# One instruction list exchanged for another: gated linear attention and a gated feed-forward on one core

## The chip, the cores and the metric

One core of a Trainium2 chip runs the whole program. The metric is the time of one execution on the device in microseconds (us). The kernel before took 240.67 us as the median of three runs (240.0 to 240.79).

## The reference

The first half is a linear attention with a complex decay for every channel, over 4 batches, 8 heads, 768 tokens and 48 channels a head. The second half is a gated feed-forward block on the 3072 tokens of 384 channels that come out of it.

```python
mag = np.sqrt(a_re * a_re + a_im * a_im)
scale = np.minimum(mag, 0.999) / (mag + 1e-06)
a_re_n, a_im_n = (a_re * scale, a_im * scale)
for t in range(S):                                   # per batch and head, state S is 48 x 48
    new_re, new_im = ar * S_re - ai * S_im, ar * S_im + ai * S_re
    S_re, S_im = new_re + outer(k[t], v[t]), new_im
    y[t] = q[t] @ S_re
x = y as [tokens, 384]
out = x + sigmoid(x @ w_res) * ((gelu(x @ w_gate) * (x @ w_val)) @ w_out)
```

## The kernel before

The tokens of a batch are cut into six chunks of 128. A **unit** is one or two (batch, chunk) blocks of the same chunk that are worked on together. There are 14 units: P0 and P1 hold one block each of chunk 0, P2 two; P3 to P10 hold two blocks each of chunks 1 to 4; P11 holds two of chunk 5, P12 and P13 one each. A unit p goes through three stages, and the names below are P3, A3, F3 for the stages of unit 3.

**Prepare (P).** SP loads ar, ai, q, k, v (`load`, L420, 192 KB for one block). The decay is summed over the tokens in logarithm and angle. ACT takes the logarithm of ar (`ln`, L442, tile la) and its inverse (`exp`, L443, tile t), t is multiplied by ai (`tai`, L445), squared (`sq`, L448 on ACT, L450 elsewhere, tile s), ACT takes the logarithm of 1 + s (L451), DVE adds it to la and caps it (L452, L456). TensorE (PE) sums la over the tokens with a triangular matrix (L406 in fp32 for units 0 to 2; L402 in two narrower pieces for the others, which need `lv`, L460, tile ll, and `tl`, L517). ACT turns the sums into exp and exp of the negative (L487 to E, L488 to Ei). The angle is ACT's arctangent of t (`atan`, L497); the last angle of the chunk before comes to it by a small DMA (`carry`, L503, L509); PE sums it, `round` (L524 on ACT, L527 on DVE) and `fr` (L529) bring it into range, `abs` (L536 on ACT, L538 on DVE), and ACT takes sine and cosine (`sin`, L542, tile CS). q times E and k times Ei (`qe`, L548, tiles Qe, Ke) times CS (`feat`, L553) are the features, transposed on PE with a copy out of PSUM (L569; `cpT`, L377 on ACT, L378 elsewhere), from unit 6 on by DMA (`dT`, L562). `vcast` brings v into bf16; `mrd`, `mrc` and `Mc` bring the last row of E to the state's layout (L492, L377 or L378, tiles mr, M).

**Attend (A).** PE multiplies features (`qk`, L610), DVE masks the product (`am`, L615), PE multiplies it with v and adds the state's share (`av`, L626, L628), `x` copies the result, `kv` (L642), `U`, `Gf`, `Gb`, `Gbc` (L665, L672, L678, L685) carry the state on.

**Forward (F).** x is transposed on PE with a copy (L708, `cpX`, tile xT), from unit 10 on by DMA (`dX`, L702). PE multiplies with the gate and the value weights (L726, tiles wg, wv: six groups of 12 matmuls for one block, twelve groups of 6 for two), ACT takes the gelu (L736), DVE multiplies (`h`, L737, tile hb), PE multiplies with the output weights (`out`, L761) and the residual gate (L748, ACT's tanh L751), DVE multiplies (`ot`, L765), `otx` adds x (L768), SP stores (L770).

Thirty groups of four matmuls on constants (`warm`, L777) stand among PE's work in the front. The weights are loaded in 16 pieces issued by POOL (L384; wg and wv in six pieces each).

ACT computes from one table at a time: logarithm and exp ("L"), arctangent and sine ("T"), gelu and tanh ("G"). Each change is an ACT_TABLE_LOAD (L785).

All 1418 steps are recorded first and numbered in the order in which the code records them. A table `PLACE` says for some steps by their number on which engine they run, and a list `ORDER` says in which order all are issued:

```python
def place(default):
    return PLACE.get(len(plan.steps), default)
...
for j in order:
    t = self.steps[j]
    ...
    x.index = min(range(x.bufs), key=lambda i: row[i])
    ...
    if t.act is not None and t.act != table:
        table = t.act
        load(table)
    ins = t.fn()
```

An engine works through its steps in the order of the list and waits at each for what it needs. Buffers, PSUM banks (8) and table loads follow from the list too.

Of the kernel before, what the change touches and what calls it, by code (L numbers as in the profile page):

```python
# [47 lines left out]
    54: "POOL", 65: "DVE", 67: "DVE", 70: "POOL", 77: "DVE", 80: "ACT", 120: "POOL", 128: "ACT", 133: "DVE", 144: "ACT",  # L48
    146: "ACT", 152: "DVE", 157: "ACT", 190: "DVE", 191: "DVE", 202: "DVE", 208: "DVE", 210: "DVE", 218: "ACT", 220: "DVE",
    224: "DVE", 233: "DVE", 239: "DVE", 242: "DVE", 245: "DVE", 247: "ACT", 303: "POOL", 307: "POOL", 315: "DVE", 319: "POOL",  # L50
    322: "DVE", 324: "DVE", 326: "DVE", 330: "POOL", 336: "DVE", 355: "DVE", 420: "DVE", 421: "POOL", 425: "POOL", 433: "ACT",
    436: "POOL", 439: "DVE", 441: "DVE", 443: "DVE", 447: "POOL", 457: "DVE", 458: "ACT", 460: "ACT", 466: "DVE", 475: "DVE",
    482: "ACT", 538: "POOL", 542: "POOL", 550: "ACT", 553: "POOL", 558: "DVE", 560: "DVE", 564: "POOL", 570: "DVE", 574: "DVE",
    577: "ACT", 589: "DVE", 592: "DVE", 640: "DVE", 667: "ACT", 670: "POOL", 673: "DVE", 675: "DVE", 677: "DVE", 680: "POOL",
    681: "POOL", 690: "ACT", 696: "DVE", 702: "DVE", 753: "DVE", 780: "ACT", 783: "POOL", 790: "DVE", 794: "POOL", 801: "ACT",
    809: "DVE", 815: "DVE", 818: "DVE", 822: "DVE", 823: "DVE", 881: "POOL", 885: "POOL", 893: "ACT", 899: "DVE", 901: "DVE",
    903: "DVE", 906: "POOL", 907: "POOL", 916: "ACT", 931: "DVE", 935: "DVE", 936: "DVE", 1009: "POOL", 1016: "DVE",
    1019: "POOL", 1020: "POOL", 1027: "DVE", 1035: "DVE", 1044: "POOL", 1049: "ACT", 1084: "DVE", 1104: "DVE", 1120: "POOL",
    1127: "DVE", 1130: "POOL", 1131: "POOL", 1140: "ACT", 1146: "DVE", 1158: "POOL", 1213: "DVE", 1227: "POOL", 1232: "DVE",
    1237: "POOL", 1238: "POOL", 1245: "ACT", 1251: "DVE", 1307: "DVE", 1318: "POOL", 1325: "POOL", 1326: "POOL", 1331: "ACT",  # L60
    1337: "DVE", 1357: "DVE", 1367: "POOL", 1371: "POOL", 1377: "POOL", 1381: "DVE", 1384: "POOL", 1390: "ACT", 1416: "DVE",
}
ORDER = [
# [754 lines left out]
```

## Time and profile before

| | |
|---|---|
| time, median of three runs | 240.67 us |
| the profiled execution, its own time | 240.8 us |
| its span, first to last instruction | 238.9 us |
| granted TensorE clock, mean | 0.996 |
| PE, DVE, ACT, POOL busy | 228.7, 205.2, 203.1, 131.3 us |
| DMA moved | 40.55 MB, mean 170 GB/s |

A view of the profile names a group of instructions by line, engine, operation and tiles. "A <- B" in a view of waits says that A sat idle until B had ended. The chain is followed back from the last instruction, at each step to what released it. Matmuls are pipelined, so that PE's busy time says little by itself; the distance from one matmul to the next says more.

### The profile page before, as it was taken

Reading aid. Unit: us, or ns where it says so; the run is one execution under the profiler, and the core shown is the slowest. Engines: PE = TensorE matmul, PEld = TensorE weight load, DVE = VectorE, ACT = ScalarE, POOL = GpSimd, SP = SyncE. Lnnn points to the kernel's source line nnn. Section 1 sums busy time; section 2 is a strip of 40 time slices with the busy share of each in tenths; the row PEclk is TensorE's granted clock in tenths of the full one; section 3 lists DMA queues with packets and bytes.
Section 4 is the critical chain, followed back from the end, with each engine's and each line's share of the span. In section 5 each row is a group of like instructions: output and inputs, shape, how many; then the busy total and the mean of one; then the engine's idle time right before and its main releaser. Section 6 shows DMA issues by size and latency. Waiting matters only on the chain.

```text
span 238.9 us, 6460 instructions
## 1 busy us (share of the span) xinstructions
PE 228.7 (96%) x2513; PEld 180.8 (76%) x2513; DVE 205.2 (86%) x366; ACT 203.1 (85%) x327; POOL 131.3 (55%) x145
## 2 busy tenths in 40 slices
PE   6996889999999999999999999999999999999992
PEld 4874678887878878868778778777778687788961
DVE  3267998999979999999999999999999989686353
ACT  4769999899999999998999999999989989934320
POOL 2506696344884675893953956825738636250110
PEclk9999999999999999999999999999999999999998
DMA  7999999999999899994989999969979496563102
GB/s 145 211 216 173 195 206 219 215 174 224 184 204 189 190 188 216 188 213 93 204 177 176 221 212 177 243 126 193 219 95 220 94 179 151 104 102 115 43 0 99
DMA packets 164798, 40.55 MB, mean 170 GB/s; under 512 B 158240, under 2 KB 164768, under 8 KB 164768
## 3 DMA queue, kind: packets, MB, share of 16 engines
q1 hardware_dynamic: 160320, 36.25, 76.2%
q0 software_dynamic: 4448, 3.90, 10.0%
q8 instruction: 19, 0.31, 0.5%
q14 instruction: 11, 0.09, 0.1%
HBM read 31.26 MB, written 4.72 MB: 151 GB/s over the span
## 4 chain that ended last, share of the span: by engine, by line
PE 81%; DVE 9%; ACT 3%; POOL 2%; DMA 2%; issue 1%; POOLq 0%; DVEq 0%; ACTq 0%
PE pb L726 33%; PE pb L761 18%; PE pb L777 6%; PE pb L402 5%; PE pb L748 4%; PE pb L610 4%; PE pb L569 3%; DMA KT<-fK 2%; PE pb L626 2%; DVE hb L737 2%; PE pb L628 2%; PE pb L406 1%; PE pb L642 1%; PE pb L708 1%; DVE am L615 1%; DVE fK L553 1%
## 5 line engine op out<-in xcount | busy, mean ns | idle before, releaser
L726 PE MATMUL pb<-xT,wv 128*128 128x256 bf16 (+1 forms) x504 | 56.0, 257 | 0.0
L785 ACT ACT_TABLE_LOAD x42 | 53.9, 1283 | 1.4 <-PEq L802 0.7
L737 DVE SCALAR_TENSOR_TENSOR hb<-hb,pb 128x512 bf16<-128x512 bf16 x72 | 47.7, 682 | 7.9 <-PE pb L726 5.7
L761 PE MATMUL pb<-wo,hb 128*128 128x384 bf16 x288 | 54.3, 326 | 0.0
L726 PE MATMUL pb<-xT,wg 128*128 128x256 bf16 (+1 forms) x504 | 53.7, 257 | 0.2
L736 ACT ACTIVATE hb<-pb 128x512 bf16<-128x512 f32 x72 | 39.8, 602 | 15.8 <-PE pb L726 15.4
L726 PEld LDWEIGHTS <-wg 128*128 128x128 bf16 x504 | 43.3, 98 | 6.9 <-DVE xT L378 0.4
L726 PEld LDWEIGHTS <-wv 128*128 128x128 bf16 x504 | 42.6, 98 | 5.7
L761 PEld LDWEIGHTS <-hb 128*128 128x128 bf16 x288 | 26.5, 97 | 13.8
L768 POOL TENSOR_TENSOR ot<-ot,x 128x384 f32<-128x384 f32 x19 | 17.2, 909 | 33.3 <-DVE ot L765 20.3
L615 DVE TENSOR_TENSOR am<-pb,mask 128x512 bf16<-128x512 f32 x48 | 31.2, 683 | 1.0 <-PE pb L610 0.8
L548 POOL TENSOR_TENSOR Ke<-k,Ei 128x768 bf16<-128x768 f32 (+1 forms) x10 | 17.3, 1732 | 5.6 <-DVE Qe L548 4.8
L777 PE MATMUL pb<-tri,ident 128*128 128x256 bf16 x120 | 17.3, 305 | 2.4 <-POOL tri masks.py:66 2.4
L765 DVE SCALAR_TENSOR_TENSOR ot<-sg,pb 128x384 f32<-128x384 f32 x24 | 13.1, 548 | 5.3 <-PE pb L761 4.6
L777 PEld LDWEIGHTS <-ident 128*128 128x128 bf16 x120 | 12.9, 109 | 6.1 <-issue 1.6
L610 PE MATMUL pb<-QT,KT 96*128 96x128 bf16 x192 | 16.8, 219 | 0.2
L452 DVE SCALAR_TENSOR_TENSOR la<-s,la 128x768 f32<-128x768 f32 (+1 forms) x14 | 11.7, 839 | 6.0 <-ACT s L451 5.8
L517 POOL TENSOR_TENSOR tl<-t 128x768 f16<-128x768 f32 (+1 forms) x10 | 13.3, 1330 | 6.5 <-DVE la L456 3.6
L548 POOL TENSOR_TENSOR Qe<-q,E 128x768 bf16<-128x768 f32 (+1 forms) x8 | 12.1, 1511 | 7.5 <-DVE Ke L548 5.4
L610 PEld LDWEIGHTS <-KT 96*128 96x128 bf16 x192 | 12.9, 97 | 3.6 <-DMA KT<-fK 0.5
L748 PE MATMUL pb<-wr,xT 128*128 128x384 bf16 x72 | 15.5, 326 | 0.0
L445 POOL TENSOR_TENSOR t<-t,ai 128x768 f32<-128x768 f32 (+1 forms) x7 | 11.8, 1692 | 2.4 <-issue 1.4
(95 smaller groups left out, 450.4 us busy)
## 6 DMA issues: line engine op xcount, KB each, us to landing
ar<-in_a_re_dram SPq DMA_DIRECT2D x24, 192.0 KB, 3.7
ai<-in_a_im_dram SPq DMA_DIRECT2D x24, 192.0 KB, 3.9
q<-in_q_dram SPq DMA_DIRECT2D x24, 192.0 KB, 3.8
vf<-in_v_dram SPq DMA_DIRECT2D x24, 192.0 KB, 3.8
k<-in_k_dram SPq DMA_DIRECT2D x24, 192.0 KB, 3.7
out_dram<-ot SPq DMA_DIRECT2D x24, 192.0 KB, 2.7
wv<-in_moe_w_val_dram POOLq DMA_DIRECT2D x6, 192.0 KB, 5.4
wg<-in_moe_w_gate_dram POOLq DMA_DIRECT2D x6, 192.0 KB, 5.8
```

The costliest lines, as they stand in the source:

```text
L517: add(e10, "tl", lambda: on[e10].tensor_tensor(out=F("tl"), in0=F("t"), in1=top("t") if HV else F("th"), op=OP.subtract), [s["t"]] if HV e ...
L548: add(e13, "qe", lambda g=g, src=src, mag=mag, e13=e13: on[e13].tensor_tensor(out=T(g + "e")[:, 0:n * H].rearrange("p x u d -> p (x u d)") ...
L610: nc.tensor.matmul(out=view()[:, h, :], lhsT=kT.tile[0:DD, u * H // 2 + h, :], rhs=qT.tile[0:DD, u * H // 2 + h, :], start=True, stop=True)
L615: add("DVE", "am", lambda u=u, am=am, view=view: nc.vector.tensor_tensor(out=am.tile[:, u * H // 2:(u + 1) * H // 2, :], in0=view(), in1=m ...
L726: nc.tensor.matmul(out=o_.at(y, nb, n * 128)[:, u, :], lhsT=w_[:, k_, (nb * m + u) * 128:(nb * m + u + 1) * 128], rhs=xt.tile[:, k_, 0:n]. ...
L736: add("ACT", "gelu", lambda gp=gp, hv=hv: nc.scalar.activation(out=hv(), in_=pv(gp), func=AF.Gelu), gs, [hh], sz, "G")
L737: add("DVE", "h", lambda vp=vp, hv=hv: nc.vector.scalar_tensor_tensor(out=hv(), in0=hv(), scalar=0.5, in1=pv(vp), op0=OP.mult, op1=OP.mult ...
L748: nc.tensor.matmul(out=rp.at(y, DM), lhsT=xt.tile[:, k_, j, :], rhs=wr[:, k_, :], start=(k_ == 0), stop=(k_ == KF - 1))
L761: nc.tensor.matmul(out=op_.at(0, DM), lhsT=hb[k_ // per].tile[:, (u * n + j) * 128:(u * n + j + 1) * 128], rhs=wo[:, k_, :], start=(k_ == ...
L768: add(e8, "otx", lambda s=s, i=i, ot=ot, e8=e8: on[e8].tensor_tensor(out=ot.tile, in0=ot.tile, in1=s["x"].tile[:, i].rearrange("p h d -> p ...
L777: nc.tensor.matmul(out=spare.at(0, 256), lhsT=ident, rhs=tri[:, :].bitcast(BF), start=True, stop=True)
L785: plan.run(ORDER, lambda table: nc.scalar.preload_act_table_set(ACT_SETS[table]), lambda ins, prev: tc.add_manual_dep(ins.ins, prev.ins.na ...
```

## The change

`PLACE` and `ORDER` are replaced by other tables. The steps, their number, their buffers and their code stay. In the text of the kernel one line falls away, so every line after the tables has a number smaller by one (L785 becomes L784).

```diff
 PLACE = {
-    54: "POOL", 65: "DVE", 67: "DVE", 70: "POOL", 77: "DVE", 80: "ACT", 120: "POOL", 128: "ACT", 133: "DVE", 144: "ACT",
...
+    53: "POOL", 54: "DVE", 62: "ACT", 65: "DVE", 67: "DVE", 70: "POOL", 77: "DVE", 78: "ACT", 120: "DVE", 128: "ACT",
...
 ORDER = [
-    46, 51, 4, 112, 23, 52, 1, 17, 13, 12, 47, 53, 54, 8, 117, 55, 118, 25, 10, 15, 6, 9, 19, 56, 181, 16, 11, 2, 113, 119,
...
```

92 steps run on another engine. DVE then has 363 of the steps (361 before), ACT 287 (285), POOL 131 (135); ACT loads a table 42 times in both.

Three places are shown as the built programs have them. The first is ACT's front, from unit 0's exponentials to its first sines; la, t, s, E, Ei and CS are the tiles named above, 384 wide for units 0 and 1, 768 for unit 2. Before:

```order
L487 ACTIVATE E<-pb 128x384
L524 ACTIVATE fr<-pb 128x384
L451 ACTIVATE s<-s 128x768
L488 ACTIVATE Ei<-pb 128x384
L487 ACTIVATE E<-pb 128x384
L785 ACT_TABLE_LOAD
L497 ACTIVATE t<-t 128x768
```

Now:

```order
L486 ACTIVATE E<-pb 128x384
L442 ACTIVATE t<-la 128x768
L487 ACTIVATE Ei<-pb 128x384
L486 ACTIVATE E<-pb 128x384
L487 ACTIVATE Ei<-pb 128x384
L450 ACTIVATE s<-s 128x768
L784 ACT_TABLE_LOAD
```

Unit 1's two exponentials stood between unit 2's logarithm of s and the table load; now all four of units 0 and 1 stand ahead of that logarithm, and the load follows it.

The second place is POOL's front, around unit 3's tai (t<-t,ai), its sq (s<-t), the pieces of wv and unit 3's two carries (t<-fr). Before:

```order
L384 DMA wr<-in_moe_w_res_dram 128x3x384
L445 TENSOR_TENSOR t<-t,ai 128x768
L492 DMA mr<-E 16x1x48
L450 TENSOR_TENSOR s<-t 128x768
L384 DMA wv<-in_moe_w_val_dram 128x768 x2
L509 DMA t<-fr 1x16x24
L384 DMA wv<-in_moe_w_val_dram 128x768
L509 DMA t<-fr 1x16x24
L384 DMA wv<-in_moe_w_val_dram 128x768
```

Now:

```order
L444 TENSOR_TENSOR t<-t,ai 128x768
L383 DMA wv<-in_moe_w_val_dram 128x768
L491 DMA mr<-E 16x1x48
L383 DMA wr<-in_moe_w_res_dram 128x3x384
L383 DMA wv<-in_moe_w_val_dram 128x768 x2
L508 DMA t<-fr 1x16x24 x2
L383 DMA wv<-in_moe_w_val_dram 128x768 x3
```

Unit 3's sq has left POOL for ACT, and the last three pieces of wv stand behind both carries.

The third place is ACT's last change from the tables of exponentials to sines, for units 12 and 13 (384 wide); sg is the tile of tanh, hb that of gelu. Before:

```order
L487 ACTIVATE E<-pb 128x384
L377 COPY x<-pb 128x384
L488 ACTIVATE Ei<-pb 128x384
L524 ACTIVATE fr<-pb 128x384
L536 ACTIVATE fw<-fr 128x384
L785 ACT_TABLE_LOAD
L542 ACTIVATE CS<-fr 128x8x48
L542 ACTIVATE CS<-fw 128x8x48 x2
```

Now:

```order
L487 ACTIVATE Ei<-pb 128x384
L486 ACTIVATE E<-pb 128x384 x2
L487 ACTIVATE Ei<-pb 128x384
L376 COPY x<-pb 128x384
L784 ACT_TABLE_LOAD
L541 ACTIVATE CS<-fr 128x8x48
L376 COPY x<-pb 128x384
L541 ACTIVATE CS<-fw 128x8x48
```

Unit 13's exponentials have come ahead of unit 12's sines, and a second copy of A11's x stands between those sines.

On SP the first loads come in another order. The two halves of unit 3's ar, loaded 9th and 14th before, are now 19th and 18th; unit 1's v, 16th before, is the 20th; no weight piece is issued by POOL before unit 0's and unit 1's q have been multiplied, where three were before.

More of the change, by code (lines that the diff above doesn't have):

```diff
@@ L47 @@
 PLACE = {
-    54: "POOL", 65: "DVE", 67: "DVE", 70: "POOL", 77: "DVE", 80: "ACT", 120: "POOL", 128: "ACT", 133: "DVE", 144: "ACT",
-    146: "ACT", 152: "DVE", 157: "ACT", 190: "DVE", 191: "DVE", 202: "DVE", 208: "DVE", 210: "DVE", 218: "ACT", 220: "DVE",
-    224: "DVE", 233: "DVE", 239: "DVE", 242: "DVE", 245: "DVE", 247: "ACT", 303: "POOL", 307: "POOL", 315: "DVE", 319: "POOL",
-    322: "DVE", 324: "DVE", 326: "DVE", 330: "POOL", 336: "DVE", 355: "DVE", 420: "DVE", 421: "POOL", 425: "POOL", 433: "ACT",
@@ L52 @@
[L52 to L60, printed above, removed]
@@ L61 @@
-    1337: "DVE", 1357: "DVE", 1367: "POOL", 1371: "POOL", 1377: "POOL", 1381: "DVE", 1384: "POOL", 1390: "ACT", 1416: "DVE",
+    53: "POOL", 54: "DVE", 62: "ACT", 65: "DVE", 67: "DVE", 70: "POOL", 77: "DVE", 78: "ACT", 120: "DVE", 128: "ACT",
+    131: "DVE", 136: "POOL", 143: "DVE", 146: "ACT", 190: "DVE", 191: "DVE", 202: "ACT", 208: "DVE", 210: "DVE", 220: "DVE",
+    222: "ACT", 224: "DVE", 282: "DVE", 307: "POOL", 315: "ACT", 319: "POOL", 322: "DVE", 326: "DVE", 336: "DVE", 340: "DVE",
+    349: "DVE", 363: "ACT", 421: "DVE", 425: "POOL", 433: "ACT", 436: "POOL", 439: "DVE", 441: "DVE", 443: "DVE", 446: "POOL",
@@ new lines @@
+    447: "POOL", 457: "DVE", 458: "ACT", 472: "DVE", 542: "POOL", 550: "ACT", 553: "POOL", 558: "DVE", 560: "DVE", 564: "POOL",
+    570: "DVE", 574: "DVE", 589: "DVE", 597: "DVE", 659: "POOL", 670: "POOL", 673: "DVE", 675: "DVE", 677: "DVE", 680: "POOL",
+    681: "POOL", 688: "DVE", 696: "DVE", 705: "DVE", 780: "ACT", 783: "POOL", 786: "DVE", 790: "DVE", 794: "POOL", 803: "ACT",
+    809: "DVE", 815: "DVE", 822: "DVE", 823: "ACT", 893: "ACT", 899: "DVE", 906: "POOL", 907: "POOL", 916: "ACT", 922: "DVE",
@@ new lines @@
+    928: "DVE", 931: "DVE", 979: "DVE", 998: "POOL", 1006: "ACT", 1009: "POOL", 1014: "DVE", 1016: "DVE", 1019: "POOL",
+    1020: "POOL", 1027: "ACT", 1035: "DVE", 1044: "POOL", 1047: "POOL", 1090: "DVE", 1104: "DVE", 1127: "DVE", 1130: "POOL",
+    1131: "POOL", 1138: "ACT", 1140: "ACT", 1146: "DVE", 1158: "POOL", 1193: "DVE", 1234: "DVE", 1237: "POOL", 1245: "ACT",
+    1292: "DVE", 1298: "DVE", 1320: "DVE", 1325: "POOL", 1326: "POOL", 1331: "ACT", 1357: "DVE", 1367: "POOL", 1377: "POOL",
+    1379: "DVE", 1381: "DVE", 1385: "POOL", 1416: "DVE",
```

123 rows, old and new, of the table ORDER are left out of this document.

## The prediction

> **What bounds the kernel now.** I read the page's busy times first, then busy time by stretches, then the chain that ended last, and last the front of each engine in order of time. The first two views:
>
> ```profile
> PE 228.7 (96%) x2513; PEld 180.8 (76%) x2513; DVE 205.2 (86%) x366; ACT 203.1 (85%) x327; POOL 131.3 (55%) x145
> ...
> 0.00:42.00 42.00, 36.37 (x368) 28.19 (x369) 28.61 (x54) 34.14 (x55) 23.21 (x39) 1.00 1.07 195
> 42.00:234.50 192.50, 192.37 (x2149) 152.62 (x2146) 175.52 (x311) 169.00 (x273) 108.06 (x107) 1.00 0.84 166
> 234.50:239.00 4.50, 0.00 (x0) 0.00 (x0) 1.11 (x2) 0.00 (x0) 0.00 (x0) 0.77 0.24 87
> ```
>
> The columns of a stretch are its length, then busy time of PE, its weight loads, DVE, ACT and POOL, the clock, the DMA's share and GB/s. From 42 to 234.5 us PE is without work for 0.13 us. Busy time alone would not prove a full PE, so I look at the distance of matmuls in the chain:
>
> ```profile
> 2.38 10.87 PE pb L777 x72
> 13.25 1.94 PE pb L406 x6
> 15.19 2.18 PE pb L777 x20
> 17.37 0.66 PE pb L406 x2
> 18.94 1.28 ACT L785
> 27.60 1.80 POOL t L445
> 29.93 1.49 POOL s L450
> 31.45 0.85 ACT t L497
> 141.39 5.24 PE pb L726 x48
> 222.25 5.36 PE pb L726 x96
> 234.55 0.57 DVE ot L765
> 235.14 0.56 DVE ot L768
> ```
>
> 96 gate and value matmuls of 128 columns take 5.36 us, 56 ns each; 48 of 256 columns take 5.24 us, 109 ns each. In mid-run and at the end the distance is the same per column: PE never starves once it is full. So the end is the moment at which PE is full, plus a fixed rest of matmuls, plus 4.4 us of tail (238.9 less 234.5), in which one `ot`, one `otx` and one store follow. Everything that can be won lies ahead of 42 us, where PE does constants (L777) for want of real work. What can be lost lies behind it, since DVE and ACT are nearly full there too:
>
> ```profile
> 24.00:204.00 180.00, 178.53 (x2036) 141.78 (x2035) 174.02 (x309) 172.47 (x279) 115.37 (x115) 1.00 0.96 186
> ...
> ACT hb L736 <- PE pb L726: 3.9, 7, 0.7
> ```
>
> From 24 to 204 us ACT is idle for 7.5 us, 3.9 of them in gelus that wait for PE (second row, the same stretch); DVE is idle for 6.0.
>
> **The change, part by part: the front.** ACT's front as traced:
>
> ```profile
> 15.99 0.84 ACT L451 ACTIVATE s<-s 128x768 f32<-128x768 f32 x1 [0.28 <-DVE s L450]
> 18.05 0.49 ACT L488 ACTIVATE Ei<-pb 128x384 f32<-128x384 f32 x1 [1.21 <-PE pb L406]
> 18.44 0.48 ACT L487 ACTIVATE E<-pb 128x384 f32<-128x384 f32 x1
> 18.94 1.28 ACT L785 ACT_TABLE_LOAD   x1
> 24.11 0.85 ACT L442 ACTIVATE la<-ar 128x768 f32<-128x768 f32 x1
> 26.68 0.84 ACT L443 ACTIVATE t<-la 128x768 f32<-128x768 f32 x1
> 35.73 0.60 ACT L736 ACTIVATE hb<-pb 128x512 bf16<-128x512 f32 x1
> ```
>
> The table load at 18.94 stands behind unit 1's two exponentials, which wait 1.21 us for PE's sum at 17.37; that sum stands behind 20 constant matmuls from 15.19 on. Now the sums of both units stand ahead of those constants, and the load follows unit 2's L451 directly. That one waits for DVE's s, not for PE. If it keeps its place it ends at 15.99 + 0.84 = 16.83, and the load, all sines, and the load of the logarithm's table behind them come 18.94 - 16.83 = **2.1 us earlier**. What must hold: unit 0, now the second, has its exponentials done by 16 us. Ahead of its sum stand thirteen of PE's thirty groups of constants, eighteen before, and on ACT two table loads, as before.
>
> Unit 3 follows. Before, its exp stands six instructions behind its ln (24.11 and 26.68); POOL's tai (27.60) and sq (29.93, 1.49 us) and ACT's arctangent (31.45) hang on it. Now exp follows ln, and sq runs on ACT, where a 768 wide instruction takes 0.84. So this piece is not late in any case and I carry the 2.1 us through: arctangent's end 31.45 + 0.85 = 32.3 becomes 30.2.
>
> PE cannot use all of it, since it also needs the weights, and POOL issues them:
>
> ```profile
> 34.69 1.23 POOL L384 DMA_DIRECT2D wv<-in_moe_w_val_dram  x1
> ...
> L384 POOL DMA_DIRECT2D wv<-in_moe_w_val_dram x6 | 5.2, 868 | 0.0
> L509 POOL DMA_DIRECT2D t<-fr x4 | 3.5, 866 | 1.6 <-ACT t L497 1.6
> ...
> DMA packets 28879, 7.72 MB, mean 193 GB/s; under 512 B 26965, under 2 KB 28876, under 8 KB 28876
> ```
>
> The last piece of wv is issued by 34.69 + 1.23 = 35.9. Now it stands behind both carries, which wait for the arctangent: 30.2 plus five issues of 0.87 = 34.5. That is 1.4 us earlier, and **1.4 us is my gain for PE**. The ends: nothing, if the DMA is the limit (7.72 MB moved in the first 40 us, and its share of 1.07 in the first 42 says that it never rested), and 2.1 if PE follows ACT. I take the issue's time, since it is the row nearest to what PE waits for.
>
> One rule of the Trainium skill speaks against this part. The row first: the clock was granted in full from PE's first busy stretch on, and the longest pause of PE behind that is this:
>
> ```profile
> PE pb L406 <- ACT t L497: 1.2, 1, 1.2
> ```
>
> A pause of 1.2 us costs no clock. The Trainium skill, "TensorE: Matmul & The Clock Gate", table of what matters for your kernels, says that an idle gap of about 3 us between bursts brings the clock to half. Now only ten of the thirty constant groups stand ahead of the first sum, and the front's pauses fall elsewhere. By the row nothing is lost; by the rule a long pause costs a stretch at half clock. It is the third rival below.
>
> **The change: the work of the full engines.** Where the 92 steps went, counted by duration:
>
> ```profile
> L448 ACT ACTIVATE s<-t 128x768 f32<-128x768 f32 x5 | 4.2, 838 | 0.0
> L377 ACT COPY KT<-pb 96x1024 bf16<-96x1024 bf16 x3 | 3.0, 1003 | 0.4 <-PE pb L569 0.4
> L377 ACT CAST x<-pb 128x384 bf16<-128x384 f32 x10 | 4.8, 477 | 0.8 <-PE pb L628 0.5 <-PE pb L626 0.3
> ...
> L548 DVE TENSOR_TENSOR Qe<-q,E 128x768 bf16<-128x768 f32 x5 | 4.8, 952 | 0.0
> L378 DVE CAST x<-pb 128x384 bf16<-128x384 f32 x14 | 7.6, 551 | 0.4 <-PE pb L628 0.3
> L378 DVE COPY KT<-pb 96x1024 bf16<-96x1024 bf16 x7 | 4.8, 682 | 0.4 <-PE pb L569 0.4
> ```
>
> ACT: four more of the 768 wide kind (+3.4), two fewer of the 1024 wide copies (-2.0), as many of the 384 wide and of the tiny ones: **+1.4 us**. DVE: one more of 0.95, two fewer of 0.55, two more of 0.68, and one more of the shortest: **+1.2 us**. POOL has four fewer and half of its span free; I cost it at nothing. PE's matmuls are the same.
>
> What counts is what stands ahead of the last units. Ahead of unit 12's second sine ACT now has four more 768 wide (+3.4), two fewer 1024 wide (-2.0), one more 384 wide (+0.5, unit 13's exponentials among them) and one more table load (+1.3): 3.2 us. Less the front's 2.1 that sine is 1.1 us late. Behind it hang DVE's features, the transposes, the mask and A12's `av`:
>
> ```profile
> 202.88 0.92 ACT L542 ACTIVATE CS<-fw 128x384 bf16<-128x384 f32 x2
> 210.32 1.28 DVE L615 TENSOR_TENSOR am<-pb,mask 128x512 bf16<-128x512 f32 x2
> 212.28 0.19 PE L626 MATMUL pb<-v,am 128*128 128x48 bf16 x1
> ```
>
> The mask ends at 211.6, PE takes `av` at 212.28: 0.7 us of slack. PE comes 1.4 earlier, so it would stop for 1.1 + 1.4 - 0.7 = 1.8 us if ACT's idle time stayed as it was. It will not: the 3.9 us in which gelus wait for PE shrink as ACT becomes the later of the two. With all of them gone the stop is nothing, with none it is 1.8. I take a third of the 3.9 as gone, 1.3: **a stop of 0.5 us**.
>
> The tail has the same last steps: `ot`, `otx`, store. I cost it at nothing: between F12's last gate group and the product that needs its gelu PE has one value group and four output groups to do meanwhile. If that cover were gone, PE would wait for one gelu (0.60, the row at 35.73) and one `h` behind it.
>
> **The sum**, against the profiled execution's 240.8 (span 238.9, 1.9 around it): -1.4 + 0.5 = -0.9, so 239.9. The median of the runs shown is 240.67, 0.1 below that execution: **239.8 us**. About 0.3% (0.7 us) is what a measurement of this kernel can tell from no change.
>
> **The rivals.** *ACT becomes the bound (slower).* Unit 3's ar comes from places 9 and 14 to 19 and 18 of the loads. If it lands late, the logarithm at 24.11 is no earlier, ACT has no front gain, and its 3.2 us stand whole ahead of unit 12's sine: A12's `av` is 3.2 - 0.7 = 2.5 late, 243.2 on the median; with half of the gelus' waits absorbed 241.2. In my sum it decides below a front gain of 1.2 us on ACT (3.2 + 1.4 - 0.7 - 1.3 - 1.4 = 1.2). For it: both full engines get more work. Against it: those waits, and loads that no longer share the DMA with three early weight pieces. Chance 0.26.
>
> *The front is worth nothing.* The DMA is full, the weights land when they did, PE is full at 42 us as before, or ACT's stop of 1.8 eats the 1.4. Then 240.4 to 241.1. Chance 0.16.
>
> *The clock.* Unit 1's v is the 20th load instead of the 16th, POOL casts it, and A1's `kv` now stands in PE's order ahead of F0's first gate matmul. If PE pauses there so long that the clock drops (1.2 us was not long enough), it is the start again: there 72 constants took 10.87 us, at the warm 0.109 each it would be 7.85, so a cold stretch costs 3.0 us. 239.8 + 3.0 = 242.8. The rule of the Trainium skill's "TensorE: Matmul & The Clock Gate" that I named above is the same mechanism; no row here shows such a drop in mid-run. Chance 0.06.
>
> *More than I count.* ACT's L451 could itself come earlier, since the DVE steps ahead of it had waits; PE follows all of 2.1 us and never stops: 238.5, down to 237.7 with another 0.8. Chance 0.1, on the fast side.
>
> **How the numbers follow.** The forecast, 238.6 to 240.3 by its bounds, has 0.42. Of that 0.06 lies within 0.7 us of 240.67. With the fast rival's 0.1, faster by over 0.3% has 0.46; with the second rival's 0.16, within 0.3% has 0.22; ACT as the bound and the clock make slower 0.32. The range takes in the fast rival whole and the slower ones up to ACT's unabsorbed case: 237.8 to 243.0; the likeliest case's own range is 238.6 to 240.3.
>
> **What would show it.** Right: ACT's first load of the sines' table near 16.8 us and its first gelu near 33.6 (35.73 less 2.1); POOL's last wv issue by 34.5; PE full from about 40 us; 0.5 us of pauses behind it, near units 9 to 12. Wrong: a first table load at 19 us, a stretch of lower clock in the front, or pauses of over 2 us behind 100 us whose releaser is DVE or ACT. If PE's pauses behind 42 us are none and the time is still not less, the front's step failed; if the front is early and the end is not, the step on ACT's list did.

## The result, and the profile after

The new kernel takes 238.93 us (median of 9 executions, 237.78 to 239.84) where the kernel before takes 240.7 (240.0 to 241.79) on the same chip: a ratio of 0.9924, 95% interval 0.9899 to 0.9949. Run again on another chip beside the experiments (`c_after`), it came to 0.9937 (0.991 to 0.9964). Ratios leave out executions that lie more than 1.5% above the fastest of their kernel; only where those are many (e8, e9, e11) the text gives the whole spread, because the ratio hides it.

The profiled execution took 238.94 us, with a span of 237.2. First the busy times, then the same stretches as before (length, busy PE, weight loads, DVE, ACT, POOL, clock, DMA share, GB/s), moved to where the tail begins:

```profile
PE 227.9 (96%) x2513; PEld 180.8 (76%) x2513; DVE 207.0 (87%) x368; ACT 203.9 (86%) x329; POOL 125.2 (53%) x141
```

```profile
0.00:42.00 42.00, 37.79 (x417) 30.09 (x418) 31.05 (x58) 35.68 (x59) 21.99 (x39) 1.00 1.06 193
42.00:232.80 190.80, 190.14 (x2103) 150.75 (x2099) 174.79 (x309) 168.21 (x271) 103.23 (x103) 1.00 0.84 168
232.80:237.30 4.50, 0.01 (x1) 0.00 (x0) 1.11 (x2) 0.00 (x0) 0.00 (x0) 0.92 0.24 87
```

These rows hold the whole account. The busy times first: ACT has 0.8 us more work than before, DVE 1.8 more, POOL 6.1 less. PE's matmuls are the same, so what PE does behind 42 us tells how far it had come by then: 192.37 us before, 190.14 now, a lead of 2.2 us. PE's idle time behind 42 us grew from 0.13 to 190.80 - 190.14 = 0.66, so 0.5 us was given back. 2.2 - 0.5 is 1.7, the difference of the spans (238.9 and 237.2). The tail is 4.4 us as before. (PE's busy time in the first row rose by 1.4 us only. Ahead of 42 us it is no clean measure of work: the same 2513 matmuls are 0.8 us shorter in total than before.)

ACT's front in order of time, then POOL's last pieces of wv:

```profile
15.07 0.84 ACT L450 ACTIVATE s<-s 128x768 f32<-128x768 f32 x1 [0.67 <-DVE s L449]
15.93 1.28 ACT L784 ACT_TABLE_LOAD   x1
21.45 0.84 ACT L441 ACTIVATE la<-ar 128x768 f32<-128x768 f32 x1
28.12 0.85 ACT L496 ACTIVATE t<-t 128x768 f32<-128x768 f32 x1
32.12 1.08 ACT L735 ACTIVATE hb<-pb 128x512 bf16<-128x512 f32 x2
```

```profile
30.32 2.27 POOL L383 DMA_DIRECT2D wv<-in_moe_w_val_dram  x3
```

The load of the sines' table is 3.0 us earlier (18.94 before), unit 3's logarithm 2.7 (24.11), its arctangent 3.3 (31.45), the first gelu 3.6 (35.73), and POOL has issued the last wv by 32.6 instead of 35.9. PE's lead is smaller than all of these. Why, its waits tell (total, times, longest), with the gelus' waits for PE from 24 to 204 us below them:

```profile
PE pb L747 <- DMA wr<-in_moe_w_res_dram: 0.9, 1, 0.9
PE pb L405 <- DVE la L455: 0.5, 1, 0.5
PE pb L725 <- DMA wv<-in_moe_w_val_dram: 0.4, 1, 0.4
PE pb L609 <- DMA QT<-fQ: 0.4, 1, 0.4
PE pb L725 <- DMA xT<-x: 0.2, 1, 0.2
```

```profile
ACT hb L735 <- PE pb L725: 2.5, 5, 0.6
```

1.3 us of the front now go to the landing of weights (wr, wv), for which PE did not wait before. The last two rows of PE are the stops behind 42 us, at unit 7 and at F10's x, and both end with a DMA transpose. In `c_after` the stop at a transpose was a different one and larger; its stretch behind 42 us and its wait there:

```profile
42.00:234.00 192.00, 190.39 (x2112) 151.01 (x2108) 174.81 (x309) 168.62 (x272) 104.35 (x105) 1.00 0.84 167
```

```profile
PE pb L609 <- DMA QT<-fQ: 1.5, 1, 1.5
```

The lead there is 192.37 - 190.39 = 2.0 us, 1.6 are lost behind it, and that execution took 240.35. So the front's gain repeats here, and how much of it is lost differs from one execution to the next. The gain can differ too: in e10 below, whose list is the same in the front, the lead was 0.7 us.

### The profile page after: what moved, and what is told of

The parts are those of the page before. It is cut to its first block, busy times and chain, and to the rows that moved or that the text cites. A ratio compares the mean times of both kernels' runs of the same rounds, so it can differ in the third digit from the quotient of the medians.

```text
span 237.2 us, 6420 instructions
## 1 busy us (share of the span) xinstructions
PE 227.9 (96%) x2513; PEld 180.8 (76%) x2513; DVE 207.0 (87%) x368; ACT 203.9 (86%) x329; POOL 125.2 (53%) x141
## 5 line engine op out<-in xcount | busy, mean ns | idle before, releaser
L725 PE MATMUL pb<-xT,wv 128*128 128x256 bf16 (+1 forms) x504 | 57.1, 257 | 0.5 <-DMA wv<-in_moe_w_val_dram 0.4
L760 PE MATMUL pb<-wo,hb 128*128 128x384 bf16 x288 | 55.2, 326 | 0.0
L444 POOL TENSOR_TENSOR t<-t,ai 128x768 f32<-128x768 f32 (+1 forms) x11 | 17.5, 1590 | 8.1 <-ACT t L442 4.5
L767 POOL TENSOR_TENSOR ot<-ot,x 128x384 f32<-128x384 f32 x16 | 14.4, 909 | 8.5 <-DVE tl L516 5.1
L547 POOL TENSOR_TENSOR Qe<-q,E 128x768 bf16<-128x768 f32 (+1 forms) x9 | 13.9, 1544 | 8.9 <-DVE s L449 7.4
L516 POOL TENSOR_TENSOR tl<-t 128x768 f16<-128x768 f32 (+1 forms) x7 | 9.6, 1367 | 12.4 <-DVE ll L459 7.9
L547 POOL TENSOR_TENSOR Ke<-k,Ei 128x768 bf16<-128x768 f32 (+1 forms) x9 | 14.8, 1641 | 0.5 <-ACT Ei L487 0.5
L552 DVE TENSOR_TENSOR fK<-Ke,CS 128x1536 bf16<-128x1536 bf16 (+1 forms) x14 | 11.7, 838 | 1.9 <-ACT fw L535 1.1
```

The source lines that it names most:

```text
L444: add(e1, "tai", lambda: on[e1].tensor_tensor(out=F("t"), in0=F("t"), in1=flat(T("ai"), n), op=OP.mult), [s["ai"]], [s["t"]], n)
L547: add(e13, "qe", lambda g=g, src=src, mag=mag, e13=e13: on[e13].tensor_tensor(out=T(g + "e")[:, 0:n * H].rearrange("p x u d -> p (x u d)") ...
L725: nc.tensor.matmul(out=o_.at(y, nb, n * 128)[:, u, :], lhsT=w_[:, k_, (nb * m + u) * 128:(nb * m + u + 1) * 128], rhs=xt.tile[:, k_, 0:n]. ...
L760: nc.tensor.matmul(out=op_.at(0, DM), lhsT=hb[k_ // per].tile[:, (u * n + j) * 128:(u * n + j + 1) * 128], rhs=wo[:, k_, :], start=(k_ == ...
L767: add(e8, "otx", lambda s=s, i=i, ot=ot, e8=e8: on[e8].tensor_tensor(out=ot.tile, in0=ot.tile, in1=s["x"].tile[:, i].rearrange("p h d -> p ...
```

## Experiments

Each ratio is that of the kernel to the kernel before, with its 95% interval. All changes are changes of the list and of the engines; the steps' code is the same. The theory at the start was that the gain is all in the front, made by ACT's earlier tables and by early loads that share the DMA with no weights, and that late transposes take some back. Its rivals: the rest of the list brings the gain; the weights set the front, so that ACT's order is worth little.

### One part of the list alone (e1, e2, e5)

```diff
-ORDER = new list
+ORDER = first 350 (e1) or 254 (e5) steps of the new list, with their engines, then the old list and engines
+ORDER = first 350 steps of the old list, with their engines, then the new list and engines   (e2)
```

> The first 350 steps of the new list with their engines (up to about 61 us in the new kernel's trace), then the old list and the old engines. Theory 'front': the whole gain is PE's lead of about 2.5 us by 48 us, and the new rest gives 0.9 us back in stops behind 48 us (2.17 against 1.26). Then this kernel keeps the lead and has the old stops: 237.8 to 238.5 us, PE's stops behind 48 us about 1.3 us. Rival 'rest': the gain comes from the list behind 61 us; then 240 to 241 us. Rival 'seam': the lead is lost where the old rest meets a front that runs ahead of its ACT and DVE; then 239 to 240 us with stops of over 2 us behind 61 us.

> The first 350 steps of the old list with their engines, then the new list and the new engines. Theory 'front': no lead at 48 us, so the sines' table loads at about 19 us, the first gelu starts near 35.7 us, and the time is 240.5 to 241.6 us. Rival 'rest': 238.5 to 239.5 us. If ACT's longer new list were the cause of the later stops, they would be larger here, since ACT comes 3 us later, and the time 241.5 to 242.5 us; if the late DMA transposes are, the stops are absorbed by the missing lead and the time is 240.5 to 241.

> The first 254 steps of the new list (to about 44 us, where PE has just become full), then the old list and old engines: an earlier cut than in the first hybrid, with 5 steps that stand on different sides of it instead of 7. 'Front': the lead of 2.5 us at 48 us is there and the old rest costs less than the new one: 237.8 to 238.6 us on a chip where the kernel before takes 240.7. 'Seam': ACT and DVE of the old rest are not ready for a PE that comes 2.5 us earlier; stops of 1 to 2 us between 44 and 70 us, and 239.5 to 240.7 us. If the stops come, they are in DVE's copies of transposes (QT, L378), as in the first hybrid.

Measured: e1 0.9978 (0.9949 to 1.0006), e5 0.9989 (0.9956 to 1.0021), e2 1.0034 (1.0004 to 1.0065). The theory 'front' has e2 right: the new rest behind the old front loses 0.8 us, 241.5 where the kernel before takes 240.7. That is above the 240.5 to 241 for late transposes and at the lower end of the 241.5 to 242.5 for ACT's longer list, so what causes the later stops is not decided by it. 'Front' has e1 and e5 wrong: the new front before the old rest brings 0.1 to 0.2% instead of 1%, 240.2 and 240.4 on the same scale. By the number alone e1 is 'rest', which e2 rules out, and e5 is 'seam'. The parts do not add: -0.2 and +0.3% make about nothing, and together they give -0.7%. From e2 to the new kernel the same front is worth 1.0%, from the kernel before to e1 0.2%. So the new front pays only with the new rest; e9, below, shows a piece of why.

### The exponentials back behind unit 2 (e3)

```diff
 PE:  -sum of la, unit 1; three groups of constants
      +nine groups of constants; sum of la, unit 1
 ACT: -E, Ei of unit 1 ... L450 of unit 2, table load
      +L450 of unit 2; E, Ei of unit 1; table load
```

> The new kernel with one thing undone: unit 1's sum of la stands behind nine groups of constants on PE again, and its two exponentials behind unit 2's logarithm of 1 + s on ACT. Theory 'ACT's order': the sines' table loads near 19 us instead of 15.93, unit 3's logarithm, arctangent and carries follow, the first gelu comes 2 to 3 us later, and the time is 240.3 to 241.2 us. Rival 'weights': the front waits for the weights (three waits of 0.9 us for wr, 0.6 for wv), which do not hang on this, so that ACT's delay is hidden: 238.6 to 239.5 us, table load late all the same.

1.0062 (1.0036 to 1.0088): slower than the kernel before, and 242.2 us on the scale of the expectation, above the range of 'ACT's order'. Two rows of ACT, one of DVE, PE's longest waits, and PE's busy time and clock in 2 us stretches:

```profile
17.99 0.49 ACT L494 ACTIVATE E<-pb 128x384 f32<-128x384 f32 x1 [2.30 <-PE pb L413]
...
18.87 1.28 ACT L792 ACT_TABLE_LOAD   x1
```

```profile
19.58 0.96 DVE L459 SCALAR_TENSOR_TENSOR la<-s,la 128x768 f32<-128x768 f32 x1 [3.72 <-POOL Qe L555]
```

```profile
PE pb L413 <- DVE la L463: 3.9, 2, 3.3
```

```profile
21.00:23.00 2.00, 1.72 (x3) 1.14 (x4) 0.89 (x3) 2.00 (x5) 1.31 (x2) 0.53 1.12 220
23.00:25.00 2.00, 2.00 (x9) 1.03 (x9) 2.00 (x5) 1.97 (x3) 1.85 (x4) 0.62 0.67 97
```

The table load is at 18.87 as in the kernel before, and the DMA does not hide it: 'weights' is out. The loss against the new kernel is 3.0 to 3.3 us, more than the lead of 2.2 us that was there to lose, because PE has used up its constants by then and stands still for 3.3 us. It waits for unit 2's la, and by the trace DVE sat idle ahead of that until POOL's Qe had ended, which needs the late E. When PE goes on, the clock is granted at 0.53 and 0.62 in the two stretches. If it is either full or half, that is (0.47 + 0.38) x 2 / 0.5 = 3.4 us at half clock. That is the prediction's rival of the clock, made by undoing the step that avoids it. The Trainium skill, "TensorE: Matmul & The Clock Gate", "Why this matters for your kernels", puts the limit at an idle gap of about 3 us. The 3.3 us here lie above it, but the measured limit is lower: a pause of 2.1 us cost the clock too (e8, below), while 1.5 us in `c_after` and 1.7 us in e6 cost none.

### Early pieces of weights (e7)

```diff
 POOL: tai of unit 0
+      three pieces of wg and wv (issued at 7.7 to 9.6 us)
       ...
-      the same three pieces (22.7, 23.3 and 25.6 us in the new kernel)
```

> The new kernel with three pieces of the weights (192 KB... each of the L384 kind) issued by POOL behind unit 0's tai at about 8 us, as in the kernel before, instead of at 22 to 26 us. 'Uncontested loads': the first loads of ar, ai, q and k share the DMA with them, the sines' table loads 0.5 to 1.5 us later than 15.93, and the time is 0.5 to 1.5 us longer, 239.4 to 240.4. 'Weights': the DMA is full all through the front, so the same bytes in another order cost nothing there, and the later pieces land 1 to 2 us earlier: PE's waits for wr and wv go and the time is 237.6 to 238.6.

1.0054 (1.0022 to 1.0086). What the two DMA queues moved from 8 to 16 us (packets, MB, share), first in the new kernel, then in e7; q1 carries what SP issues, q0 what POOL issues:

```profile
q1 hardware_dynamic: 9057, 1.71, 109.7%
```

```profile
q1 hardware_dynamic: 5370, 1.02, 67.3%
q0 software_dynamic: 432, 0.59, 42.9%
```

0.59 MB of weights cost the loads 0.69 MB. DVE's row shows whom that hits, PE's wait and its clock what follows:

```profile
15.79 0.96 DVE L452 TENSOR_TENSOR t<-t,ai 128x768 f32<-128x768 f32 x1 [3.48 <-DMA ai<-in_a_im_dram]
```

```profile
PE pb L413 <- DVE la L463: 3.3, 1, 3.3
```

```profile
20.00:24.00 4.00, 3.40 (x8) 1.84 (x9) 2.89 (x7) 3.98 (x7) 2.99 (x5) 0.57 1.12 216
```

Unit 2's tai waits 3.5 us for ai, its sum comes late, PE stands for 3.3 us and the clock falls to 0.57. So the kernel needs both: the new order on ACT, and loads that the weights do not disturb. 'Uncontested loads' is right in kind; the time is 2.8 us above the new kernel's instead of 0.5 to 1.5. The clock was not in it: 0.43 x 4 / 0.5 = 3.4 us at half clock again, in which 1.7 us of work are lost. Since e3 and e7 both end in such a pause, they show that each part is needed, but not what each would be worth without the clock.

### Unit 3's sq back on POOL (e6)

```diff
+    303: "POOL",
```

> The new kernel with unit 3's sq back on POOL: 1.49 us there instead of 0.84 on ACT, at the same place of the list, ahead of four pieces of weights. 'ACT and tables set the front': unit 3's arctangent and carries come 0.6 us later and PE loses 0.3 to 0.7 us: 239.2 to 239.7 on a chip where the new kernel takes 238.9. 'Weights set the front': POOL issues them 1.5 us later and PE loses 1 to 1.5 us: 239.9 to 240.4. 'Neither': ACT is relieved by 0.84 us later on and nothing is lost: 238.6 to 239.0.

Without an entry in `PLACE` this step runs on ACT, as in the new kernel. 0.9951 (0.992 to 0.9982) beside 0.9937 (0.991 to 0.9964) for the new kernel on the same chip. The two can't be told apart, though 0.9951 is where 'ACT and tables' begins (0.995 to 0.997); the 1 to 1.5 us of 'weights' would be 0.998 to 1.0, at or beyond the end of the interval. Its waits say that the weights did come later, PE waiting 1.7 us for wr instead of 0.9 (0.6 in `c_after`):

```profile
PE pb L756 <- DMA wr<-in_moe_w_res_dram: 1.7, 1, 1.7
```

### Unit 4's loads later (e4)

```diff
 SP: -408, 409, 411, 410 (unit 4's ar, ai), 294, 295, 297, 296 (unit 3's q and k)
     +294, 295, 297, 296, 408, 409, 411, 410
```

> The new kernel with the four loads of unit 4's ar and ai moved behind the loads of unit 3's q and k in SP's list, so that the DMA is free for the weights between 25 and 39 us. Theory 'weights': PE's waits for wr and wv in the front (1.5 us) shrink and the time falls by 0.5 to 1.3 us, to 237.6 to 238.4. Rival 'unit 4': its logarithm comes late and ACT or PE waits for unit 4's features instead; 239 to 240.5 us. Rival 'queue': the weights' order on their own queue sets when they land, whatever else the DMA moves: 238.7 to 239.1, the same waits.

1.0415 (1.0373 to 1.0458), the largest loss of all, and outside every theory's numbers; 'unit 4' had the mechanism. What the loads are up against is seen in the new kernel's queues from 24 to 28 us, with the median time from issue to landing:

```profile
q0 software_dynamic: 445, 0.61, 83.7%
q1 hardware_dynamic: 1217, 0.23, 34.5%
...
vf<-in_v_dram SPq DMA_DIRECT2D x1, 192.0 KB, 17.2
ar<-in_a_re_dram SPq DMA_DIRECT2D x1, 192.0 KB, 14.0
```

While the weights go through, a load of 192 KB needs 14 to 17 us instead of some 4. Moving the four loads back by four places thus put unit 4's ar far behind: SP issues it at 40.5 us instead of 26.4. e4's rows of ACT, PE and clock show the price:

```profile
52.52 0.84 ACT L449 ACTIVATE la<-ar 128x768 f32<-128x768 f32 x1 [10.28 <-DMA ar<-in_a_re_dram]
```

```profile
PE pb L755 <- ACT hb L743: 9.6, 1, 9.6
```

```profile
56.00:58.00 2.00, 1.80 (x8) 1.05 (x8) 0.96 (x1) 1.98 (x5) 0.11 (x1) 0.50 1.13 224
...
60.00:62.00 2.00, 2.00 (x24) 1.51 (x22) 1.90 (x3) 1.70 (x5) 0.00 (x0) 1.00 1.05 200
```

ACT works in the order of its list, so the gelus behind that logarithm waited too, and PE for them, until 56.2 us. The clock was still at half for the first 3.6 us behind that.

### Two loads moved ahead of unit 3's ar (e8, e9)

```diff
 SP: ..., 50,
+    116 (unit 1's v), 183 (half of unit 2's q),
     290, 291 (unit 3's ar),
-    116, 185, 183, ...
+    185, ...
```

The text of the expectations calls loads 290 and 291 unit 3's ai; they are its ar, which the logarithm needs.

> The new kernel with two loads moved in SP's list, ahead of unit 3's ai: unit 1's v and the second half of unit 2's q, which now stand last before the pieces of weights take the DMA (from 21 us on the loads move 120 to 300 KB in 4 us, against 800 to 860 before). 'Edge of the weights': what decides the front is whether unit 2's q has landed before the weights start; in the two hybrids of the front it landed at 36 us, in the new kernel by 31.7. Then the median falls by 0.2 to 0.8 us against the new kernel's 0.9937 and 0.9924 of the kernel before, to 0.990 to 0.993, and the scatter shrinks. 'Not limiting': in the new kernel unit 2's q waits for nobody, so nothing changes: 0.992 to 0.994. 'Unit 3': its ai lands too late for tai on POOL, weights and arctangent follow, 0.995 to 1.000.

> The hybrid of the new list's first 254 steps and the old rest (0.9989 of the kernel before) with the same two loads moved ahead. 'Edge of the weights': the hybrid lost its lead because unit 2's q landed at 36 us; with q early PE's wait of 3.4 us for unit 2's features goes, PE has done 25.5 to 26.5 us of work by 48 us instead of 21.9, and the time is 0.990 to 0.994. 'Seam': the old rest cannot use a front that comes 2.5 us earlier; q lands early, the pauses move behind 48 us, and the time stays at 0.997 to 1.000.

e8: 0.9938 (0.9905 to 0.9971) for five of the twelve executions; the other seven took 243.2 to 248.3 us, and the median of all is 243.85. e9: 1.0044 (1.0009 to 1.008) with five of twelve left out; the whole spread is 240.3 to 247.1, the median 243.44. Neither median came as expected, and the mistake about ar is the first reason: unit 3's logarithm comes late, and behind it in ACT's list stands a cast of v for which PE now waits. PE's wait in e8 (2.1 in e9 too), and its stretches from 24 to 30 and 30 to 36 us:

```profile
PE pb L633 <- ACT v L384: 2.1, 1, 2.1
```

```profile
24.00:30.00 6.00, 3.85 (x46) 3.13 (x45) 3.01 (x7) 5.77 (x13) 4.02 (x5) 0.87 1.18 210
30.00:36.00 6.00, 6.00 (x93) 5.26 (x92) 5.48 (x9) 5.45 (x8) 3.99 (x7) 0.85 1.22 210
```

(0.13 + 0.15) x 6 / 0.5 is 3.4 us at half clock once more, behind a pause of 2.1 us. This was one of the five short executions, at a mean clock of 0.989 (the five: 0.989 to 1.0). The seven long ones have 0.979 to 0.986. One stretch of 3.4 us at half clock takes 0.007 off the mean, so the longest, at 0.979, lost the clock more than once; where, no trace shows.

How close unit 3's ar is to deciding the front is best seen on ACT's logarithm of it, in the new kernel (its loads and their landing, the row at 21.45 above having no wait), in `c_after`, e10 and e8:

```profile
L419 SPq DMA_DIRECT2D ar<-in_a_re_dram x2: 697/790/882, 15.6 to 16.6; - x2
...
DMA to landing us min/median/max: 3.7/3.7/3.8
```

```profile
21.74 0.84 ACT L441 ACTIVATE la<-ar 128x768 f32<-128x768 f32 x1 [0.41 <-DMA ar<-in_a_re_dram]
```

```profile
22.37 0.84 ACT L449 ACTIVATE la<-ar 128x768 f32<-128x768 f32 x1 [0.74 <-DMA ar<-in_a_re_dram]
```

```profile
24.18 0.84 ACT L449 ACTIVATE la<-ar 128x768 f32<-128x768 f32 x1 [2.88 <-DMA ar<-in_a_re_dram]
```

In the profiled execution ar lands at 16.6 + 3.8 = 20.4, 1.1 us ahead of the logarithm; with SP's list unchanged there, it was 0.4 and 0.7 us late in two others; two places later, 2.9. A late ar is how the prediction's first rival begins. By the prediction's sum that rival decides below a front gain of 1.2 us on ACT, with the logarithm behind 24.11 - 1.2 = 22.9, and the new kernel was 1.5 us away from it. Its price is not shown: in e8's profiled execution the logarithm is as late as in the kernel before (24.18 and 24.11), the time was still 240.22 where that takes 240.76, and behind 42 us PE waits nowhere for ACT. What the long executions of e8 wait for is not known.

e9 also shows the seam of e1 and e5. PE's stretch from 58 to 63 us in e9, then in the kernel before:

```profile
58.00:63.00 5.00, 4.36 (x49) 3.24 (x48) 4.52 (x8) 4.60 (x7) 3.26 (x3) 1.00 1.05 208
```

```profile
58.00:63.00 5.00, 5.00 (x63) 4.27 (x62) 4.99 (x9) 4.27 (x6) 3.30 (x4) 1.00 1.14 220
```

Here PE loses 0.6 us, waiting for DVE's features, where the old kernel loses nothing. That fits an old rest laid out for a PE that comes later, and may be a part of what e1 and e5 lost. The other part stays open. In their own profiled executions, which are among the longest of each and are left out of the ratios, unit 2's q comes late (DVE's Qe starts at 36.0 and 36.6 us, 31.7 in the new kernel), and PE waits 2.5 and 3.4 us for it. In e9 that wait is gone and the time is no better, so q alone is not the cause.

### Two stores behind the transposes (e10)

```diff
 SP: 800 (transpose),
-    518 (store), 798, 797, 799 (transposes)
+    798, 797, 799, 518
 ...
-    980 (store), 1159 (transpose of x)
+    1159, 980
```

> The new kernel with two stores of results moved behind DMA transposes that stood right behind them in SP's list: F4's behind unit 7's last transpose, F8's behind F10's second transpose of x. In three traces a transpose that is issued within 0.1 us of a store takes 1.9 to 2.45 us, all others 1.2 to 1.9, most 1.3. 'Transposes': the two stops of PE behind 130 us that end with a transpose (0.56 and 0.40 us in the profiled execution) shrink to under 0.2 each, and the time falls by 0.4 to 0.9 us: 0.989 to 0.992 of the kernel before. 'Only shifted': PE then waits for DVE or ACT at the next place, nothing changes: 0.992 to 0.994. 'Stores': the late stores hold up the loads behind them; slower, 0.995 to 0.998.

SP's issues (start, us) in the new kernel, then in e10:

```profile
126.17 0.52 SPq L769 DMA_DIRECT2D out_dram<-ot  x1
126.75 2.44 SPq L561 DMA_TRANSPOSE KT<-fK  x1
...
184.70 0.53 SPq L769 DMA_DIRECT2D out_dram<-ot  x1
185.32 2.35 SPq L701 DMA_TRANSPOSE xT<-x  x1
```

```profile
126.79 2.63 SPq L569 DMA_TRANSPOSE KT<-fK  x2
...
186.13 3.66 SPq L709 DMA_TRANSPOSE xT<-x  x2
```

```profile
PE pb L617 <- DMA QT<-fQ: 1.2, 1, 1.2
```

Without the store right ahead, the two KT of unit 7 take 2.63 together, where one took 2.44; the pair of x takes 3.66 in place of 1.19 + 2.35 and is not helped. In the kernel before that pair takes 4.67 with a load ahead of it and no store, so for x the store is not the cause. The stops at unit 7 and at F10 are gone (0.4 and 0.2 us in the list above, where the expectation has 0.56 and 0.40). The one that is left (last row, from 120 us on) is that of `c_after`, at unit 9. The time is 0.9905 (0.9869 to 0.9942): the best ratio of all, as 'transposes' expected it, but by 6 executions whose interval holds the new kernel's 0.9924 and 0.9937 as well. It is not shown to be faster. The profiled execution is the longest of the six, 241.23, and shows that the front's lead can be small with the same list:

```profile
42.00:235.00 193.00, 191.56 (x2134) 152.15 (x2131) 175.95 (x312) 169.24 (x273) 104.30 (x105) 1.00 0.85 167
```

192.37 - 191.56, less 0.1 that PE still does behind 235 us, is a lead of 0.7 us. In this execution ar came 0.7 us late; that this is the cause is not shown.

### Unit 3's ar earlier (e11)

```diff
 SP: 115,
+    290, 291 (unit 3's ar), 116 (unit 1's v),
     184 (half of unit 2's k), 50 (unit 0's v),
-    290, 291, 116, ...
```

> The new kernel with the two stores of the run before moved back, and with three loads moved ahead of the first half of unit 2's k in SP's list: unit 3's ar (both halves) and unit 1's v. 'ar sets the front': in the new kernel unit 3's logarithm waits for ar by nothing to 0.7 us, depending on how long one load's issue takes (0.9 to 2.4 us), and by 2.9 where ar stood two places later; with ar 1.8 us earlier the logarithm follows the table load in every course, at 21.3 to 21.5 us. The scatter shrinks, and with the stops at the transposes gone the time is 0.986 to 0.990 of the kernel before (237.4 to 238.4 where that takes 240.8). 'Another load': what is pushed back (unit 2's k, unit 0's v) lands too late before the weights take the DMA; unit 0's v holds ACT's cast at 23.7, PE pauses for over 2 us and the clock falls; 0.995 to 1.005, or some executions of 243 and more. 'Nothing': 0.990 to 0.993.

```profile
20.58 1.28 ACT L792 ACT_TABLE_LOAD   x1
21.88 0.84 ACT L449 ACTIVATE la<-ar 128x768 f32<-128x768 f32 x1
```

The two stores stand as in e10 in this run. The logarithm now follows the table load without a wait, as expected, and that did not help: 0.9916 (0.9876 to 0.9956) for five of the twelve executions, 241.9 to 243.2 us for the other seven, and a median of 241.89, above the 240.92 of the kernel before beside it. 'Another load' comes nearest, but which one is not seen: the profile is of one of the five. Of the seven long executions four have a mean clock of 0.986 to 0.992, and three have 0.996 to 1.0, so the clock is not all of it. Of the two kernels compared, and of all that were tried, none is reliably better than the new one; its 21 executions lie between 237.8 and 241.4 us without a second group.

## Why the prediction was right

It said 239.8 us, range 237.8 to 243.0; 238.93 came. The gain was forecast at 0.9 us and came to 1.8. By its steps:

- *Nothing to win but ahead of 42 us.* Right for the time: the lead of 2.2 us is there at 42 us. Read as a statement on the list it would be wrong: the first 350 steps alone bring 0.2% (e1).
- *The table load 2.1 us earlier, at 16.83.* Right in kind, too small: 15.93, 3.0 earlier. The term took unit 2's L451 at its old place (15.99); it came at 15.07, for the work ahead of it had waits that went as well. That is what the fast rival had named, with a chance of 0.1. e3 shows that this step is needed.
- *Unit 3 carries it through.* Right, with more: the first gelu is 3.6 us earlier instead of 2.1. Of the 1.5 us, 0.9 are the load's; the logarithm is 2.7 earlier, the arctangent 3.3, so the exp that follows directly and sq on ACT add 0.6. e6 does not tell sq's own share from zero.
- *PE gains 1.4 us, with POOL's last issue.* This term was mis-sized: 2.2 us measured. POOL's last issue came 3.3 us earlier, so by the step's own rule PE would have gained 3.3; it did not, since wr and wv land 1.3 us after PE needs them. Issue and landing are not the same thing when the DMA is full.
- *A stop of 0.5 us.* The size was met, 0.53, and the cause was not. The forecast had A12's `av` wait for unit 12's second sine, which ACT's longer list was to bring 1.1 us late. It came 1.2 us earlier than the 202.88 of before:

```profile
201.67 0.53 ACT L541 ACTIVATE CS<-fw 128x384 bf16<-128x384 f32 x1
```

- *The stops that came.* They are at DMA transposes instead, of unit 7 and of F10's x, and in `c_after` of unit 9. The gelus' waits for PE shrank from 3.9 to 2.5, as much as was assumed (1.3). The number came out by chance, and `c_after` has 1.6 us in its place.
- *The work of the full engines.* ACT got 0.8 us more (forecast 1.4), DVE 1.8 more (forecast 1.2). Neither bounds the new kernel.
- *ACT becomes the bound.* Not in the profiled execution. Its first step, a late ar of unit 3, did come in the neighbours, 0.4 to 2.9 us; its price of 0.5 to 2.5 us, in waits for ACT near the end, was seen in no trace.
- *The clock.* No drop in the new kernel, and a real price nearby: pauses of 2.1 to 3.3 us were followed by 3.4 us at half clock (e3, e7, e8). That is 1.7 us of work besides the pause; the 3.0 us taken from the start were too much for the clock's part.
- *The front is worth nothing.* Out: 2.2 and 2.0 us of lead in two executions of the new kernel.

## What to carry to other kernels

When the busiest engine is full but for the front, count how much work it has done by a fixed time; that one difference, less the idle time behind it, gives the gain of that execution without any chain. A list that is planned as a whole can't be cut in two and its halves priced: the halves came to -0.2 and +0.3% here, the whole to -0.7%. Before a load is moved back, look whether it passes the point at which the large transfers start: what lands before it in 4 us needs 14 to 17 behind it, and an in-order engine passes that wait on to all.

## What the runs showed of the hardware

- Weights issued by POOL crowd out loads issued by SP. In the new kernel q1 moves 1.71 MB in the 8 us from 8 to 16, when it has the DMA for itself, and 0.23 MB in the 4 us from 24 to 28, beside 0.61 MB of q0. The packets there are 1217 to 445, so q1's are some 190 bytes and q0's 1.4 KB. The Trainium skill, "DMA: Bandwidth & Descriptors", "Queues, rings and completion order", says that each DMA engine takes turns between queues packet by packet. Turns of small packets against large ones would give the small ones few bytes. The direction agrees; the counts, 2.7 to 1, are not equal turns, but the page's packet is a bundle of descriptors, and the trace's packets may not be the ones meant.
- A pause of PE of 2.1 us (e8) or 3.3 us (e3, e7) is followed by 3.4 us at half the clock, as worked out above from the clocks of the stretches. Behind one of 9.6 us it was 0.50 at 56 to 58 us and 1.00 from 60 on (e4). Pauses of up to 1.7 us cost none (e6, whose clock is 1.00 through the first 42 us).
- The issue of a DMA transpose on SP takes 1.2 to 1.4 us in most cases here; single ones took up to 2.44. Two long ones stood right behind a store; without it one of the two pairs got shorter and the other did not, so that a store lengthens it is not shown in general.
- The same loads in another order can split the executions of one kernel into two groups (e11: 238.1 to 239.7 and 241.9 to 243.2; e8: 238.6 to 240.6 and 243.2 to 248.3). In e8 the long group has the lower mean clock throughout, in e11 only in part. What throws an execution into one or the other was not found.
